# Attention and feed-forward on one core: a shared reciprocal in the prologue, a maximum set free of a remainder, and a copy moved to ScalarE

## The chip, the cores and the metric

The kernel runs on one core of a Trainium2 chip. The metric is the device time of one execution in microseconds (us), taken as the median of several executions. Five engines share the core and run their own instruction streams in order: TensorE (PE, with its weight loads shown apart as PEld), VectorE (DVE), ScalarE (ACT), GpSimd (POOL, hardly used here) and SyncE (SP), whose queue issues most of the DMA transfers. An engine that waits for a semaphore holds everything behind it in its own stream.

## The reference: attention through 32 memory slots, then a gated feed-forward

The inputs have 8 batch elements, 8 heads, 576 positions and head size 64; `phi` has 32 columns for each head and position. Cut to what matters:

```python
a = exp(phi - max(phi, axis=2));  a = a / (sum(a, axis=2) + 1e-9)     # max and sum over the 576 positions
k_m = einsum('bhsm,bhsd->bhmd', a, k);  v_m = einsum('bhsm,bhsd->bhmd', a, v)
scores = scale * (q @ k_m.T)                                          # 576 x 32 for each head
attn = exp(scores - max(scores, axis=-1));  attn = attn / (sum(attn, axis=-1) + 1e-9)
x = (attn @ v_m), heads side by side                                  # 4608 x 512
h = x @ w_in;  out = (h * sigmoid(h)) @ w_out                         # 512 -> 2048 -> 512
```

## The kernel before, in words

The kernel goes through the eight batch elements, numbered 0 to 7. `v_m` and `w_in` are multiplied first (`p_mm`, giving `pm`), so that a batch element's hidden row `h` is attention weights times `pm`. Every float32 operand of a large product is split in a rounded high part and a remainder, both in a 32-bit format that PE takes at full rate, and three products (high x high, high x low, low x high) are summed. In the text "g" is the activated hidden block: `gbuf` holds it as float32, and `gparts` holds its high part (a CAST on DVE in batch elements 0 and 1, line 718) and its remainder (a subtraction on DVE, line 720).

For batch elements 0 and 1 the hidden dimension is done in 16 slots of 128 columns. In a slot PE does `ffn1` (12 products into the PSUM tile `h`, line 701), ACT applies SiLU in two pieces (`gbuf`, line 728; `gleft`, line 730), DVE splits the result, and PE then does the second product of the slot before (`acc`, line 746). `h` has one buffer: `ffn1` of the next slot waits until ACT has read `h` to the end, that is until `gleft`.

Into these slots, as events, is woven the attention of the next batch element. In batch index 1 the next one is element 2, and its events are: the maximum over `phi` (`phi_max`, lines 258 to 261, then `phi_fold`, lines 286 to 304, ending in the tile `am`), its subtraction (`phi_sub`, lines 312 and 315), the exponential on ACT, the products with `k` and `v` (`e_mm`), the turn of their result (`e_tr`, two PE transposes and two copies into `kvT`, lines 368 and 369), and the scores. Batch index 1 also prepares, eight times, sums of weight blocks for a Strassen-like scheme that the later batch elements use (`w_forms`: a sum of 1024 columns on DVE at line 814, four small ones at lines 818 to 821, a rounding on ACT at line 835, a remainder on DVE at line 836).

The order on DVE is found by the tile scheduler, which moves an instruction ahead where it sees it ready. A dependency without a semaphore (`behind`) pins an instruction after another on the same engine. In batch index 1, events whose function stands in the list `late` are pinned behind `last_split[-1]`, the subtraction that makes the remainder of this slot's g. PE's order is the program's throughout, ACT's from batch index 1 on, and in the prologue both DVE and ACT follow the program.

The prologue does the attention of element 0 with nothing to hide behind. Its softmax over 32 slots is done in two parts, u = 0 (512 columns) and u = 1 (640 columns), of one tile `fsc`: maximum, subtraction, exponential on ACT (line 576), sum (line 580), addition of 1e-9 and reciprocal (lines 581 and 582), product (line 586), then PE transposes (`f_back`, tile `firsta`, line 593). Between them stand steps that put the first weights together from 64-bit words (`w_conv`: step "s" is a shift on DVE, line 176, step "a" an addition on DVE, line 178), and groups of spare PE products (`keep_warm`, line 80) that write to a tile nobody reads.

Of the kernel before, what the change touches and what calls it, by code (L numbers as in the profile page):

```python
# [16 lines left out]
ALU = mybir.AluOpType  # L17
AX = mybir.AxisListType

P = 128  # L20
# [28 lines left out]
def attn_ffn_kernel(  # L49
# [313 lines left out]
    def e_tr(b):  # L363
        pt = beside_h(P) if b <= 2 else banks(b)
        t = sb.tile([P, 2, NR, M], F32, tag="kvT", name=f"kvT{b}", bufs=2)
        for kind in range(2):
            nc.tensor.transpose(pt[kind][:, :P], kvn[:, kind].rearrange("p g d -> p (g d)"), ident)
        nc.vector.tensor_copy(t[:, 0].rearrange("p r m -> p (r m)"), pt[0][:, :P])
        nc.scalar.copy(t[:, 1].rearrange("p r m -> p (r m)"), pt[1][:, :P])
        at[b]["kvT"] = t  # L370

# [183 lines left out]
    def f_sc(u):  # L555
        return f_part(u, "sc", 2 * S)

    def f_groups(x):
        return x.rearrange("p (n m) -> p n m", m=M)
# [16 lines left out]
        nc.scalar.activation(f_sc(u), f_sc(u), AF.Exp, scale=SCALE)  # L576

    def f_sum(u):
        sm = f_part(u, "sm", 2 * S // M)
        nc.vector.tensor_reduce(sm, f_groups(f_sc(u)), op=ALU.add, axis=AX.X)  # L580
        nc.vector.tensor_scalar(sm, sm, EPS, None, op0=ALU.add)
        nc.vector.reciprocal(sm, sm)

# [222 lines left out]
    def w_forms(j, step):  # L806


        if step == 0:
            while len(kept) < 3 * j + 3:  # L810
                keep(*homes_left.pop(0))
            f = at[0]["forms", j] = sb.tile([P, 2, DMODEL], F32, tag="cva", name="wf", bufs=1)
            c = slice(2 * j, 2 * j + 2)
            i = nc.vector.tensor_tensor(f, as_f32(wo_hi[:, c]), as_f32(wo_lo[:, c]), op=ALU.add)  # L814
            if j < 3:
                behind(i.ins, last_kvn[0] if j == 2 else last_split[-1])
            b11, b12, b21, b22 = (f[:, k, q * Q : (q + 1) * Q] for k in range(2) for q in range(2))
            nc.vector.tensor_tensor(b11, b12, b11, op=ALU.subtract)
            nc.vector.tensor_tensor(b12, b22, b12, op=ALU.add)
            nc.vector.tensor_tensor(b22, b22, b11, op=ALU.add)  # L820
            nc.vector.tensor_tensor(b21, b22, b21, op=ALU.subtract)
            return
        f = at[0]["forms", j].rearrange("p k (q f) -> p (k q) f", q=2)
        t1 = sb.tile([P, 1, DMODEL], F32R, tag="cva1", name="t1", bufs=1)
        runs = [[t1, 0, 1]]
        for u in range(3 * j, 3 * j + 3):
            t, i = kept_at[u]
            if t is runs[-1][0]:
                runs[-1][2] = i + 1
            else:  # L830
                runs.append([t, i, i + 1])
        n = 0
        for t, i, e in runs:
            src, to = f[:, n : n + e - i], t[:, i:e]
            nc.scalar.activation(to[:, :, :Q], src, AF.Copy)
            nc.vector.tensor_tensor(to[:, :, Q:], src, to[:, :, :Q], op=ALU.subtract)  # L836
            n += e - i
        load(saved[j], as_f32(t1[:, 0]))
# [313 lines left out]
    with in_order(DVE, ACT) as last:  # L1152
        load_phi(0)
        nc.scalar.activation(tiny[:, :1], ident[:, :1], AF.Exp)
        load_kv(0)
        for c in LOADS.split():
            if c[0] == "Q":
                load_q(0, int(c[1]), True)
            elif c[0] == "L":
                load_next(True)  # L1160
            else:
                w_load((c[0], 0), int(c[1]), True)
        keep_warm(idle, 10)
        phi_max(0, (0,))
        phi_allmax(0, (0,))
        phi_max(0, (1,))
        keep_warm(idle, 3)
        phi_sub(0, (0,))
        phi_allmax(0, (1,))
        phi_sub(0, (1,))  # L1170
        for p in range(2):
            phi_exp(0, (p,))
        keep_warm(idle, 2)
        e_mm(0)
        w_conv(I0, 0, "pc")
        keep_warm(idle, 3)
        f_tr()
        f_vt()
        w_conv(I0, 0, "s")
        keep_warm(idle, 2)  # L1180
        f_scores(0)
        f_scores(1)
        f_copy(0)
        w_conv(I0, 0, "a")
        f_turn(0)
        f_copy(1)
        f_max(0)
        f_turn(1)
        f_sub(0)
        spare = ps.tile([P, 512], F32, tag="acc", name="spare", bufs=NI)  # L1190
        keep_warm(spare, 3)
        f_exp(0)
        w_conv(I0, 1, "pc")
        f_max(1)
        f_sub(1)
        f_exp(1)
        nc.scalar.activation(tiny[:, :1], ident[:, :1], AF.Silu)
        keep_warm(spare, 13)
        f_sum(0)
        f_norm(0)  # L1200
        w_conv(I0, 1, "sa")
        f_back(0)
        f_sum(1)
        w_conv(O0, 0, "p")
        f_high(0)
        w_conv(O0, 0, "c")
        keep_warm(spare, 3)
        bg = p_mm(0, 0, CW, False)
        keep_warm(spare, 5)
        p_split(0, 0, CW, bg, (0,))  # L1210
        w_conv(I1, None, "p")
        f_norm(1)
        f_back(1)
        f_low(0)
        w_conv(O0, 0, "s")
        f_high(2)
        p_split(0, 0, CW, bg, (1,))
        f_high(1)
        w_conv(O0, 0, "h")
        f_low(1)  # L1220
        f_low(2)
        w_conv(O0, 0, "a")
        w_conv(I1, None, "c")
        h = ffn1(0, 0, low_last=True)
        g32 = silu(0, 0, h)
        w_conv(I1, None, "s")
        gs = split(g32, steps=(2,))
        w_conv(O0, 0, "l")
        w_conv(I1, None, "a")
        split(g32, steps=(1,), gs=gs)  # L1230
        g32 = silu(0, 1, ffn1(0, 1, bgtile()))
        w_conv(O0, 1, "pc")
        main_step(0, 0, gs, (0, 1), (0, 1))
        g1 = split(g32, steps=(0,))
        w_conv(O0, 1, "s")
        p_mm(0, CW, CW)
        w_conv(O0, 1, "h")
        main_step(0, 0, gs, (0, 1), (2,))
        main_step(0, 0, gs, (2, 3))
        split(g32, steps=(1,), gs=g1)  # L1240
        w_conv(O0, 1, "al")
        prev = ("main", 0, 1, g1)
# [46 lines left out]
    for b in range(B):  # L1289
        if b == 1:  # L1290
            whole.close()
            ctx.enter_context(in_order(ACT))
        for s in range(NFC if b > 1 else 0):
            t, j = divmod(s, NP)
            h = ffn1s(b, t, j)
            part = forms(b, t, j, h)
            run(b, s)
            finish(range(NI))
            prev = ("st", b, t, j, part)
        for fc in range(NFC if b < 2 else 0):  # L1300
            if b == 0 and fc < 2:
                for part in range(2):
                    for fn, a in events.pop((b, fc + part / 2), []):
                        fn(*a)
                continue
            h = ffn1(b, fc, low_last=b == 1 and fc == 0)
            gs = split(silu(b, fc, h), steps=(2, 1) if fc == NFC - 1 else (0, 1))
            for part in range(2):
                if b == 0:
                    finish((2 * part, 2 * part + 1))  # L1310
                traced = nc.cur_bb.bb.instructions
                n = len(traced)
                late = set()
                for fn, a in events.pop((b, fc + part / 2), []):
                    m = len(nc.cur_bb.bb.instructions)
                    fn(*a)
                    if fn is phi_max or b and fn in (s_max, s_sub, s_sum, s_norm, s_back, s_low):
                        late.update(i.name for i in list(nc.cur_bb.bb.instructions)[m:])
                if b == 0:
                    for i in list(nc.cur_bb.bb.instructions)[n:]:  # L1320
                        if i.engine == ACT:
                            behind(i, last_silu[-1])
                        elif i.engine == DVE and (fc > 10 or i.name in late):
                            behind(i, last_split[-1])
                for i in list(nc.cur_bb.bb.instructions)[n:] if b else ():
                    if i.engine == DVE and i.name in late:
                        behind(i, last_split[-1])
            if b:
                finish(range(NI))
            prev = ("main", b, fc, gs)  # L1330
        if b % 2:
            for n in range(NLS):
                gs = left_split(b, n)
                run(b, NFC + n)
                finish((0, 1, 2, 3))
                prev = ("left", b, n, gs)
# [56 lines left out]
```

## Time and profile before

| what | value |
|---|---|
| median of 3 runs | 682.2 us (681.66 to 682.36) |
| the profiled execution | 681.68 us, of which the profile spans 679.9 us |
| PE busy | 666.5 us, 98% of the span |
| DVE, ACT busy | 518.6 us (76%), 370.1 us (54%) |
| granted PE clock over the execution | 0.997 |

PE is busy nearly always, so the row that matters is not a share but the list of the few places where PE stands still. A row of the timeline gives the start, the busy time, the engine, the line, the operation, the tiles, the count, and in brackets the idle time of that engine just before with what ended it. The granted clock is a column of the table by windows: 1.00 is full speed.

### The profile page before, as it was taken

To read this page: it belongs to the slowest core of one execution; us is meant where nothing else is said; L and a number is where in the kernel's file an instruction comes from. 1 tells how busy PE (TensorE), PEld (TensorE's weight loads), DVE (VectorE), ACT (ScalarE), POOL (GpSimd) and SP (SyncE) were. 2 spreads that over 40 slices of the span, in tenths; PEclk is the share of its full clock that TensorE was granted. 3 is DMA by queue.
4 is the path that set the end of the run, shared out by engine and by line. 5 is a ranking of instruction groups with operands and counts; after the bars stand their busy time and mean duration, and the time that the engine had idled before them with its cause. 6 is when DMAs were issued, how large, how long until landed. Compare 5 with 4: busy or idle time off the path is not lost.

```text
span 679.9 us, 14538 instructions
## 1 busy us (share of the span) xinstructions
PE 666.5 (98%) x5792; PEld 589.8 (87%) x5792; DVE 518.6 (76%) x1093; ACT 370.1 (54%) x685; POOL 0.7 (0%) x6
## 2 busy tenths in 40 slices
PE   7999999899999999999999999999999999999997
PEld 3687778687879998999988999899996999889996
DVE  4997897888958688868877678887977668867653
ACT  3878684433535646554654646564654546554541
POOL 0000000000000000000000000000000000000000
PEclk9999999899999999999999999999999999999999
DMA  9998975133271443243430524216431204210001
GB/s 340 368 339 275 322 294 204 50 110 99 89 252 47 183 157 124 79 143 126 173 132 16 184 73 169 101 35 243 156 125 34 86 2 156 95 45 17 32 1 47
DMA packets 37907, 93.92 MB, mean 138 GB/s; under 512 B 4688, under 2 KB 21456, under 8 KB 34256
## 3 DMA queue, kind: packets, MB, share of 16 engines
q1 hardware_dynamic: 36816, 90.22, 38.1%
q10 hardware_dynamic: 1024, 2.77, 1.0%
q8 instruction: 46, 0.75, 0.5%
q14 instruction: 21, 0.17, 0.1%
HBM read 77.22 MB, written 15.73 MB: 137 GB/s over the span
## 4 chain that ended last, share of the span: by engine, by line
PE 85%; DVE 4%; issue 1%; ACT 1%; DMA 0%; ACTq 0%; DVEq 0%
PE sum L893 36%; PE h L854 22%; PE acc L746 7%; PE h L701 5%; PE lsum L977 5%; PE bg L649 3%; PE accleft L746 2%; PE bg L335 1%; PE bg L382 1%; PE h L335 1%; PE pacc L649 1%; DVE wf L814 1%; DVE kept L836 0%; DMA out<-o 0%; DVE gparts L720 0%
## 5 line engine op out<-in xcount | busy, mean ns | idle before, releaser
L854 PE MATMUL h<-aparts,pm 128*128 128x288 f32 x1152 | 168.5, 295 | 0.0
L854 PEld LDWEIGHTS h<-aparts,pm 128*128 128x128 f32 x1152 | 157.4, 188 | 0.5
L868 ACT ACTIVATE gbuf<-h 128x512 f32<-128x512 f32 x96 | 57.3, 597 | 116.8 <-PE h L854 114.2
L893 PE MATMUL sum<-wo_hi,aparts 128*128 128x256 f32 x384 | 102.3, 289 | 0.0
L893 PE MATMUL sum<-kept,aparts 128*128 128x256 f32 x576 | 100.1, 282 | 0.0
L893 PE MATMUL sum<-wo_lo,aparts 128*128 128x256 f32 x384 | 100.0, 282 | 0.0
L873 DVE TENSOR_TENSOR gbuf<-gbuf 128x256 f32<-128x256 f32 x96 | 40.6, 423 | 69.0 <-ACT gbuf L868 68.6
L882 ACT ACTIVATE aparts<-gbuf 128x512 fp32r<-128x512 f32 x86 | 54.4, 633 | 62.1 <-DVE gbuf L877 62.1
L746 PE MATMUL acc<-wo_hi,gparts 128*128 128x512 f32 x256 | 85.1, 397 | 0.0
L893 PEld LDWEIGHTS sum<-kept,aparts 128*128 128x128 f32 x576 | 82.5, 191 | 0.0
L893 PEld LDWEIGHTS sum<-wo_hi,aparts 128*128 128x128 f32 x384 | 72.7, 189 | 9.8 <-ACT gleft L870 7.5
L884 DVE TENSOR_TENSOR gparts<-gbuf,aparts 128x512 fp32r<-128x512 f32 x86 | 59.6, 693 | 19.6 <-ACT aparts L882 19.6
L893 PE MATMUL sum<-wo_hi,gparts 128*128 128x256 f32 x384 | 73.2, 281 | 0.0
L893 PEld LDWEIGHTS sum<-wo_lo,aparts 128*128 128x128 f32 x384 | 73.1, 190 | 0.0
L893 PE MATMUL sum<-kept,gparts 128*128 128x256 f32 x288 | 65.5, 282 | 0.0
L701 PEld LDWEIGHTS h<-aparts,pm 128*128 128x128 f32 x372 | 52.3, 190 | 10.5 <-ACT gleft L730 4.0
L701 PE MATMUL h<-aparts,pm 128*128 128x288 f32 x372 | 56.8, 302 | 4.0 <-ACT gleft L730 2.9
L893 PEld LDWEIGHTS sum<-wo_hi,gparts 128*128 128x128 f32 x384 | 59.4, 190 | 0.0
L746 PEld LDWEIGHTS acc<-wo_hi,gparts 128*128 128x128 f32 x256 | 48.3, 190 | 11.6 <-issue 1.0
L872 ACT ACTIVATE aparts<-gbuf 128x384 fp32r<-128x384 f32 x96 | 50.4, 525 | 0.0
L746 PE MATMUL acc<-wo_lo,gparts 128*128 128x512 f32 x128 | 49.6, 395 | 0.4 <-DVE wo_lo L182 0.4
L893 PEld LDWEIGHTS sum<-kept,gparts 128*128 128x128 f32 x288 | 47.9, 190 | 0.0
(225 smaller groups left out, 956.9 us busy)
## 6 DMA issues: line engine op xcount, KB each, us to landing
win<-win_saved SPq DMA_DIRECT2D x24, 1024.0 KB, 5.0
kv<-in_kv SPq DMA_DIRECT2D x28, 516.0 KB, 5.0
q<-in_q SPq DMA_DIRECT2D x16, 576.0 KB, 6.3
raw<-in_w_in SPq DMA_DIRECT2D x14, 512.0 KB, 7.6
raw<-in_w_out SPq DMA_DIRECT2D x6, 1024.0 KB, 6.5
win_saved<-win SPq DMA_DIRECT2D x4, 1024.0 KB, 8.6
phi<-in_phi SPq DMA_DIRECT2D x7, 576.0 KB, 8.5
out<-oo SPq DMA_DIRECT2D x26, 128.0 KB, 1.9
```

The costliest lines, as they stand in the source:

```text
L335: nc.tensor.matmul(pt[p][M * r : M * (r + 1), :KVW], e[:, p, c, M * r : M * (r + 1)], kvt[c][:, p, r], start=c == 0, stop=False, skip_grou ...
L649: nc.tensor.matmul((bg[p][M * r : M * (r + 1)] if beside else bg[M * r : M * (r + 1), p, :w]).rearrange("p (k f) -> p k f", f=P), kvT[D * ...
L701: nc.tensor.matmul(h[:, hf, :HALF], wt[:, p, fs], a[:, p, hf * HALF : (hf + 1) * HALF], start=n[hf] == 0, stop=n[hf] == 5, skip_group_chec ...
L746: nc.tensor.matmul(acc[key], gt[:, cs], wt[:, fc], start=fc == 0 and n == 0, stop=fc == NFC - 1 and n == 2)
L854: nc.tensor.matmul(h[:, i, :HALF], wt[:, p, f : f + P], a[:, p], start=n == 0, stop=n == 5)
L868: nc.scalar.activation(gbuf[:, :MAIN].rearrange("p (i f) -> p i f", i=2), h[:, :, :w], AF.Silu)
L872: nc.scalar.activation(hi[:, :3], g[:, 1:4], AF.Copy)
L873: nc.vector.tensor_tensor(g[:, 4:6], g[:, :1].broadcast_to([P, 2, P]), g[:, 1:3], op=ALU.subtract)
L882: nc.scalar.activation(hi[:, 3:], g[:, 4:], AF.Copy)
L884: last_split.append(nc.vector.tensor_tensor(lo[:, 3:], g[:, 4:], hi[:, 3:], op=ALU.subtract))
L893: nc.tensor.matmul(sums[bank][:, place * Q : (place + 1) * Q], gt[:, k], wt, start=bank not in begun, stop=True, skip_group_check=True,)
L977: nc.tensor.matmul(sums[k], part[gt][:, 2 * i + k], wt[:, fc], start=n == 0 and i == 0 and m == 0, stop=True, skip_group_check=True,)
```

## The change

Four edits.

1. Prologue: the sums of both parts are taken first, with the shift of the next weights between them; then one addition and one reciprocal serve all 36 columns; then the products of u = 0 and u = 1, with the weights' addition between them.
2. Batch index 1: `phi_max` is no longer in the list `late` there (it still is in batch index 0), so it isn't pinned behind the remainder of g.
3. Batch index 1: the turned keys of element 2 (first copy of `e_tr`) are copied out of PSUM by ACT in place of DVE.
4. Batch index 1: the sixth `w_forms` (j = 5) is pinned behind the remainder of `pm` (`last_p[-1]`, line 679).

```diff
@@ e_tr @@
-        nc.vector.tensor_copy(t[:, 0].rearrange("p r m -> p (r m)"), pt[0][:, :P])
+        (nc.scalar.copy if b == 2 else nc.vector.tensor_copy)(t[:, 0].rearrange("p r m -> p (r m)"), pt[0][:, :P])
@@ f_sum @@
-        sm = f_part(u, "sm", 2 * S // M)
-        nc.vector.tensor_reduce(sm, f_groups(f_sc(u)), op=ALU.add, axis=AX.X)
+        nc.vector.tensor_reduce(f_part(u, "sm", 2 * S // M), f_groups(f_sc(u)), op=ALU.add, axis=AX.X)
+
+    def f_rec():
+        sm = first["sm"]
         nc.vector.tensor_scalar(sm, sm, EPS, None, op0=ALU.add)
         nc.vector.reciprocal(sm, sm)
@@ w_forms @@
-            if j < 3:
-                behind(i.ins, last_kvn[0] if j == 2 else last_split[-1])
+            if j < 3 or j == 5:
+                behind(i.ins, last_kvn[0] if j == 2 else last_p[-1] if j == 5 else last_split[-1])
@@ the prologue @@
         f_sum(0)
+        w_conv(I0, 1, "s")
+        f_sum(1)
+        f_rec()
         f_norm(0)
-        w_conv(I0, 1, "sa")
+        w_conv(I0, 1, "a")
         f_back(0)
-        f_sum(1)
         w_conv(O0, 0, "p")
@@ the loop over batch indices 0 and 1 @@
-                    if fn is phi_max or b and fn in (s_max, s_sub, s_sum, s_norm, s_back, s_low):
+                    if fn is phi_max and not b or b and fn in (s_max, s_sub, s_sum, s_norm, s_back, s_low):
                         late.update(i.name for i in list(nc.cur_bb.bb.instructions)[m:])
```

Only DVE and ACT change their order; PE's and SP's streams are the same instruction for instruction. What follows shows three places.

DVE in the prologue, before (`fsc` is the softmax tile, `fsm` its sums, `win_72` the first weights):

```order
L580 TENSOR_REDUCE fsm<-fsc 128x16
L581 TENSOR_SCALAR fsm<-fsm 128x16
L582 RECIPROCAL fsm<-fsm 128x16
L586 TENSOR_TENSOR fsc<-fsc,fsm 128x512
L176 TENSOR_SCALAR win_72<-win_72 128x512
L178 ISA win_72<-raw,win_72 128x1024
L580 TENSOR_REDUCE fsm<-fsc 128x20
L581 TENSOR_SCALAR fsm<-fsm 128x20
L582 RECIPROCAL fsm<-fsm 128x20
L586 TENSOR_TENSOR fsc<-fsc,fsm 128x640
```

and the same place now (lines are two or so further down):

```order
L579 TENSOR_REDUCE fsm<-fsc 128x16
L176 TENSOR_SCALAR win_72<-win_72 128x512
L579 TENSOR_REDUCE fsm<-fsc 128x20
L583 TENSOR_SCALAR fsm<-fsm 128x36
L584 RECIPROCAL fsm<-fsm 128x36
L588 TENSOR_TENSOR fsc<-fsc,fsm 128x512
L178 ISA win_72<-raw,win_72 128x1024
L588 TENSOR_TENSOR fsc<-fsc,fsm 128x640
```

Two instructions are gone. The product of u = 0 now stands behind the sum of u = 1, and the product of u = 1 has two instructions fewer ahead of it.

DVE at the start of batch index 1, before (`mt`, `mx` belong to `phi_max` of element 2, `pm` is the remainder of a `p_mm`):

```order
L720 TENSOR_TENSOR gparts<-gbuf,gparts 128x512
L718 CAST gparts<-gbuf 128x512
L720 TENSOR_TENSOR gparts<-gbuf,gparts 128x512
L718 CAST gparts<-gbuf 128x512
L720 TENSOR_TENSOR gparts<-gbuf,gparts 128x512
L258 TENSOR_TENSOR mt<-phi_1109 128x512
L259 TENSOR_TENSOR mx<-mt 128x256
L261 TENSOR_TENSOR mx<-mx,phi_1109 64x128
L679 TENSOR_TENSOR pm<-bg,pm 128x1024
L261 TENSOR_TENSOR mx<-mx,phi_1109 64x128
```

and now, up to the same remainder `pm`, from the same first row on (`phi_fold`'s rows between `mxt` and `am`, and `phi_sub`'s, are in the second piece):

```order
L722 TENSOR_TENSOR gparts<-gbuf,gparts 128x512
L258 TENSOR_TENSOR mt<-phi_1107 128x512
L259 TENSOR_TENSOR mx<-mt 128x256
L261 TENSOR_TENSOR mx<-mx,phi_1107 64x128
L720 CAST gparts<-gbuf 128x512
L261 TENSOR_TENSOR mx<-mx,phi_1107 64x128
L722 TENSOR_TENSOR gparts<-gbuf,gparts 128x512
```

and further down the same stream, from the end of `phi_fold` to the first `w_forms`:

```order
L304 STREAM_TRANSPOSE am<-wide 128x256
L312 TENSOR_TENSOR phi_1107<-phi_1107,am 128x512
L315 TENSOR_TENSOR phi_1107<-phi_1107,am 64x128
L720 CAST gparts<-gbuf 128x512
L312 TENSOR_TENSOR phi_1107<-phi_1107,am 128x512
L722 TENSOR_TENSOR gparts<-gbuf,gparts 128x512
L315 TENSOR_TENSOR phi_1107<-phi_1107,am 64x128
L681 TENSOR_TENSOR pm<-bg,pm 128x1024
L720 CAST gparts<-gbuf 128x512
L722 TENSOR_TENSOR gparts<-gbuf,gparts 128x512
L816 TENSOR_TENSOR wf<-wo_hi,wo_lo 128x1024
```

`phi_max` starts two splits of g earlier, `phi_fold` stands whole between the first and the second of these splits, and `phi_sub` ends ahead of the first `w_forms` (`wf`); before, three of its four instructions stood among the rows of that `w_forms`.

DVE in the tenth slot of batch index 1, before (`kvT_1652` are the turned keys of element 2):

```order
L718 CAST gparts<-gbuf 128x512
L814 TENSOR_TENSOR wf<-wo_hi,wo_lo 128x1024
L720 TENSOR_TENSOR gparts<-gbuf,gparts 128x512
L679 TENSOR_TENSOR pm<-bg,pm 128x1024
L368 COPY kvT_1652<-h 128x128
L818 TENSOR_TENSOR wf<-wf 128x256
```

and now, the copy having gone to ACT, where it stands just ahead of the copy of line 369:

```order
L720 CAST gparts<-gbuf 128x512
L722 TENSOR_TENSOR gparts<-gbuf,gparts 128x512
L681 TENSOR_TENSOR pm<-bg,pm 128x1024
L816 TENSOR_TENSOR wf<-wo_hi,wo_lo 128x1024
L820 TENSOR_TENSOR wf<-wf 128x256
```

## The prediction, made before the changed kernel ran

> **What bounds the kernel now.** I read the page first, then PE's own list of waits, then the timeline around each wait that the change touches.
>
> ```profile
> PE 666.5 (98%) x5792; PEld 589.8 (87%) x5792; DVE 518.6 (76%) x1093; ACT 370.1 (54%) x685; POOL 0.7 (0%) x6
> PE h L701 <- ACT gleft L730: 2.9, 1, 2.9
> PE firsta L593 <- DVE fsc L586: 0.7, 2, 0.5
> PE firstm L276 <- DVE cm L271: 1.2, 2, 0.8
> ```
>
> PE bounds it. It stands still only in the prologue and at a handful of places, so a change on DVE or ACT is worth what it does to those waits. The rows (engine, waited for: total, times, longest) name two that the edits touch: 2.9 us at one `ffn1` that waits for `gleft`, and the transposes of the prologue, which wait for the softmax products; a third comes below. The last row is of the prologue too: its longest wait is 0.8 us.
>
> **Edit 2, the maximum set free.** This is where the 2.9 us come from:
>
> ```profile
> 104.55 0.33 SPq L88 DMA_DIRECT2D phi<-in_phi  x1
> phi<-in_phi SPq DMA_DIRECT2D x1, 576.0 KB, 3.8
> 113.00 0.43 DVE L718 CAST gparts<-gbuf 128x512 fp32r<-128x512 f32 x1 [3.13 <-ACT gbuf L728]
> 114.14 0.68 DVE L258 TENSOR_TENSOR mt<-phi 128x512 f32<-128x512 f32 x1
> 121.71 1.22 DVE L814 TENSOR_TENSOR wf<-wo_hi,wo_lo 128x1024 f32<-128x1024 f32 x1
> 123.49 0.42 ACT L835 ACTIVATE t<-wf 128x256 fp32r<-128x256 f32 x1 [5.26 <-DVE wf L818]
> 125.93 0.84 ACT L835 ACTIVATE kept<-wf 128x768 fp32r<-128x768 f32 x1 [2.02 <-DVE wf L821]
> 127.16 0.21 ACT L730 ACTIVATE gleft<-h 128x64 f32<-128x64 f32 x1
> 115.74 1.75 PE L701 MATMUL h<-aparts,pm 128*128 128x288 f32 x12
> 120.07 1.75 PE L701 MATMUL h<-aparts,pm 128*128 128x288 f32 x12
> 127.42 2.60 PE L701 MATMUL h<-aparts,pm 128*128 128x288 f32 x12 [2.86 <-ACT gleft L730]
> 133.40 1.75 PE L701 MATMUL h<-aparts,pm 128*128 128x288 f32 x12
> 128.00:132.00 4.00, 4.00 (x16) 3.56 (x15) 3.63 (x7) 3.72 (x6) 0.00 (x0) 0.57 0.00 0
> ```
>
> Read it backwards. PE's `ffn1` at 127.42 waited 2.86 us for `gleft`. ACT was late with `gleft` because it is in order and stood first at `t`, then at `kept`, for the sums of the first `w_forms` on DVE. DVE was late with those because `mt` started only at 114.14, behind a CAST for which DVE had idled 3.13 us. Yet `phi` was there: issued at 104.55, 3.8 us to landing, at 108.35. The last row (window; busy times of PE, PEld, DVE, ACT, POOL; granted clock, 0.57) shows a second price: after the gap the clock was low.
>
> Now the new time. `mt` can start at about 108.4, when `phi` lands. Between `mt` and `wf` DVE was busy without a gap for 121.71 - 114.14 = 7.57 us. In the new order the same work stands there, and in addition two CASTs, two remainders of g, one large and two small parts of `phi_sub`:
>
> ```profile
> L720 DVE TENSOR_TENSOR gparts<-gbuf,gparts 128x512 fp32r<-128x512 f32 x32 | 22.0, 688 | 1.2 <-PE acc L746 0.5
> L312 DVE TENSOR_TENSOR phi<-phi,am 128x512 f32<-128x512 f32 x12 | 8.2, 681 | 0.0
> L315 DVE TENSOR_TENSOR phi<-phi,am 64x128 f32<-64x128 f32 x12 | 3.4, 284 | 0.2
> ```
>
> With the CAST's 0.43 that is 2 x (0.43 + 0.69) + 0.68 + 2 x 0.28 = 3.48 us, so `wf` starts at 108.4 + 7.57 + 3.48 = 119.45 in place of 121.71. From `wf` to `kept` on ACT it took 125.93 - 121.71 = 4.22 us, with 0.68 + 2 x 0.28 = 1.24 us of `phi_sub` in between that are no longer there: 3.0 us, up to 3.2 as neighbours overlap a little. `kept` starts at 122.4 to 122.6, and `gleft` ends 127.37 - 125.93 = 1.44 us later, at 123.9 to 124.1.
>
> PE, running freely, repeats a slot in 120.07 - 115.74 = 4.33 us and would issue its `ffn1` at 124.40. So `gleft` is 0.4 us early and the whole wait goes: 127.42 - 124.40 = 3.02 us. Without the gap the clock should stay up: 133.40 - 127.42 = 5.98 us for this slot become 4.33, another 1.65 us. Together **-4.67 us**.
>
> Is it given back?
>
> ```profile
> 159.47 1.22 DVE L679 TENSOR_TENSOR pm<-bg,pm 128x1024 fp32r<-128x1024 f32 x1
> 135.88 0.43 DVE L718 CAST gparts<-gbuf 128x512 fp32r<-128x512 f32 x1 [1.46 <-ACT gbuf L728]
> ```
>
> The second CAST and remainder of g now stand behind the maximum and `phi_fold`, and feed PE. Counted back from `wf` at 119.45 over what stands between (a CAST and a remainder 1.1, the remainder of `pm` 1.2, a small `phi_sub` 0.3), that remainder ends at about 116.8. PE takes it up behind the `ffn1` of 115.74, whose row ends at 117.49, so the cover is 0.7 us; beyond it a microsecond on DVE is one on PE. The remainder of `pm` ends near 118.3; its columns are first used by the `ffn1` at 124.4. Behind that slot PE is 4.67 us earlier and DVE only 2.26 + 1.24 = 3.5; the 1.2 us between them fit in DVE's idle time of 1.46 us two slots on.
>
> [...]
>
> **Edits 3 and 4, the tenth slot.**
>
> ```profile
> 157.21 1.03 ACT L677 ACTIVATE pm<-bg 128x1024 fp32r<-128x1024 f32 x1
> 157.73 1.22 DVE L814 TENSOR_TENSOR wf<-wo_hi,wo_lo 128x1024 f32<-128x1024 f32 x1
> 160.17 0.39 PE L746 MATMUL acc<-wo_hi,gparts 128*128 128x512 f32 x1
> 160.92 0.27 ACT L369 COPY kvT<-h 128x128 f32<-128x128 f32 x1 [2.68 <-DVE kvT L368]
> 161.23 1.86 PE L701 MATMUL h<-aparts,pm 128*128 128x288 f32 x12 [0.67 <-ACT kvT L369]
> ```
>
> The transposed keys lie in columns of `h`, so `ffn1` waited for both copies, and DVE reached its copy only behind `wf` and the remainder of `pm` (ended at 160.69); ACT idled 2.68 us for it. ACT is free at 158.24; two copies of 0.27 end by 158.8, long before PE is through with its products of 160.17. The wait of the last row goes: **-0.67 us**. The remainder of `pm`, at 159.47 until now, comes ahead of the 1.22 us of `wf`; and `wf`, later by as much, is next needed by ACT's `t`, which stands behind the next `gleft`, an `ffn1` away (161.23 + 1.86). So edit 4 costs nothing; without that cover it would cost up to 1.2 us.
>
> **Edit 1, the prologue.**
>
> ```profile
> 19.32 0.68 DVE L580 TENSOR_REDUCE fsm<-fsc 128x16 f32<-128x512 f32 x1
> 19.50 0.73 ACT L576 ACTIVATE fsc<-fsc 128x640 f32<-128x640 f32 x1
> 20.53 0.69 DVE L586 TENSOR_TENSOR fsc<-fsc,fsm 128x512 f32<-128x512 f32 x1
> 21.68 0.69 DVE L178 CUSTOM_DVE_ANT_0 win<-raw,win 128x1024 uint16<-128x1024 uint16 x1
> 22.29 0.81 DVE L580 TENSOR_REDUCE fsm<-fsc 128x20 f32<-128x640 f32 x1
> 23.35 0.28 DVE L582 RECIPROCAL fsm<-fsm 128x20 f32<-128x20 f32 x1
> 23.66 0.83 DVE L586 TENSOR_TENSOR fsc<-fsc,fsm 128x640 f32<-128x640 f32 x1
> 100.21 0.38 DVE L440 RECIPROCAL ssm<-ssm 128x36 f32<-128x36 f32 x1
> 17.23 3.62 PE L80 MATMUL spare<-ident 128*128 128x512 bf16 x16
> 21.37 0.63 PE L593 MATMUL firsta<-ident,fsc 128*128 128x128 f32 x4 [0.53 <-DVE fsc L586]
> 23.17 1.25 PE L80 MATMUL spare<-ident 128*128 128x512 bf16 x5
> 24.64 0.63 PE L593 MATMUL firsta<-ident,fsc 128*128 128x128 f32 x4 [0.21 <-DVE fsc L586]
> ```
>
> The second sum can start when its exponential ends (20.23) and the shift is out of the way, at 20.3. From sum to product took 23.66 - 22.29 = 1.37 us; the reciprocal of 36 columns is 0.10 longer: the product of u = 0 starts at 21.77, not 20.53, **1.24 us later**. The product of u = 1, behind it and the addition (22.29 - 21.68 = 0.6 us each), starts at 23.0, 0.6 us earlier. DVE gains, but PE is in order: its first transposes move to 22.6, and behind them stand spare products, a `p_mm` and five more spares before the second transposes. That stretch lasts at least 24.30 - 21.37 = 2.93 us (five spares at 0.226, the mean distance of the sixteen) and at most 24.42 - 21.37 = 3.05. The second transposes come at 25.5 to 25.65 in place of 24.64: **+0.9 to +1.0 us**, and the first `ffn1`, released through them, moves along. PE's list of waits has nothing long behind it until batch index 1, so I find nothing that gives it back. I take +0.9; the bounds are 0 (hidden after all) and the lost clock below.
>
> **The sum.** -4.67 - 0.67 + 0.9 = -4.44 us. The profiled execution took 681.68 us, so it becomes 677.2. It stood 0.5 us under the median of 682.2; the median becomes **677.8 us**.
>
> **Rivals.**
>
> *A wait remains at `gleft`* (13%). The margin is 0.3 to 0.5 us over some 30 DVE instructions. If these take 1.6 us more, PE waits 1.2 us, too short to lose the clock: 679.0. Against it: the sum used unshortened durations.
>
> *The clock falls in the prologue* (11%). PE would stand still from 17.23 + 3.62 = 20.85 to 22.6, 1.75 us. A gap of 2.86 us lost the clock, the 0.8 us of the first fence did not. If this one does, it costs what the other cost, 1.65 us: 679.4. [...]
>
> *`phi` lands late, and the kernel becomes slower* (5%).
>
> ```profile
> phi<-in_phi SPq DMA_DIRECT2D x7, 576.0 KB, 8.5
> ```
>
> Over all seven loads the median is 8.5 us. With it `mt` starts at 113.05 and holds the splits of g behind it: `gleft` at 128.7 in place of 127.37, the clock lost as before, the prologue's 0.9 on top: 681.68 + 1.3 + 0.9 - 0.7 = 683.2, some 683.7 as a median. It decides from a landing of about 7 us on, where the gap is again 2.9 us. Against it: the row for this very load, in a quiet queue, says 3.8.
>
> *The prologue's delay is hidden* (11%), in a later wait of PE that DVE, 0.5 us ahead by the saved pair, answers sooner: 676.9.
>
> *The order does nothing for the time* (2%): 682.2.
>
> **How the numbers follow.** The forecast gets 58%. Range 676.6 to 679.7: from the hidden prologue to the lost clock, which leaves out late `phi`, no effect and accidents. The median can tell about 0.2%, 1.4 us, from no change; below 680.8 lie the forecast and three rivals, 93%, cut to 0.90 for what I don't see; the same 0.05, slower 0.05.
>
> **What would show it.** No PE wait for `gleft` near 124 us and a granted clock of 1.00 in the four microseconds after; `mt` within a microsecond of 109 (all plus the prologue's shift); `ffn1` of the eleventh slot without a wait for `kvT`; the first transposes of the prologue near 22.6 with idle time of about 1.7 us ahead, the second near 25.5 with none. I am wrong if PE waits for `gparts` around 117, if the prologue's clock falls below 1.00, or if the second transposes are no later than 24.64.

## The result and the profile after

The changed kernel takes **677.71 us** (median of 6 executions, 676.74 to 679.49) against 682.12 us of the kernel before (6 executions, 680.09 to 682.72): a ratio of 0.9941, with a 95% interval of 0.9924 to 0.9958. The forecast was 677.8. The profiled execution of the changed kernel spans 675.9 us at a mean granted clock of 1.0, against 679.9 us at 0.997.

PE's line of the page in the changed kernel (in it the lines are two further down: `ffn1` is L703, `gleft` L732):

```profile
PE 664.9 (98%) x5792; PEld 588.8 (87%) x5792; DVE 518.2 (77%) x1090; ACT 370.3 (55%) x686; POOL 0.7 (0%) x6
```

PE is busy 1.6 us less with the same 5792 products: time that the lowered clock, 0.50 over 3.42 us of the trace of before (shown below), had added. Two waits have left the list, the 2.9 us of `ffn1` for `gleft` and its 0.7 us for `kvT`, and one has grown: the transposes of the prologue now wait 1.75 us, once, where they waited 0.7 in two pieces.

**Batch index 1.** The timeline of the changed kernel around the wait that is gone, and one row of its table by windows (window; busy times of PE, PEld, DVE, ACT, POOL; granted clock; DMA):

```profile
105.89 0.33 SPq L88 DMA_DIRECT2D phi<-in_phi  x1
109.74 0.69 DVE L258 TENSOR_TENSOR mt<-phi 128x512 f32<-128x512 f32 x1 [0.83 <-DMA phi<-in_phi]
120.79 1.22 DVE L816 TENSOR_TENSOR wf<-wo_hi,wo_lo 128x1024 f32<-128x1024 f32 x1
124.25 0.85 ACT L837 ACTIVATE kept<-wf 128x768 fp32r<-128x768 f32 x1 [1.34 <-DVE wf L823]
125.48 0.22 ACT L732 ACTIVATE gleft<-h 128x64 f32<-128x64 f32 x1
129.99 0.22 ACT L732 ACTIVATE gleft<-h 128x64 f32<-128x64 f32 x1
117.09 1.75 PE L703 MATMUL h<-aparts,pm 128*128 128x288 f32 x12
121.42 1.75 PE L703 MATMUL h<-aparts,pm 128*128 128x288 f32 x12
125.75 1.86 PE L703 MATMUL h<-aparts,pm 128*128 128x288 f32 x12
130.26 1.86 PE L703 MATMUL h<-aparts,pm 128*128 128x288 f32 x12
128.00:132.00 4.00, 4.00 (x23) 3.24 (x21) 3.86 (x10) 3.31 (x7) 0.00 (x0) 1.00 0.05 20
```

`mt` starts as `phi` lands (its bracket), 3.85 us after its issue, and everything up to `gleft` follows sooner. Seen from the `ffn1` two slots ahead of the one that waited (115.74 before, 117.09 now), `wf` starts at +3.70 in place of +5.97. The `ffn1` at 125.75 comes one free slot of 4.33 us after the one at 121.42, where it came 127.42 - 120.07 = 7.35 us after: -3.02 us. The clock stays at 1.00, where it was 0.57, and the next slot takes 130.26 - 125.75 = 4.51 us in place of 5.98: -1.47. Together -4.49 us.

But `gleft` ends at 125.70 and PE starts at 125.75: there is no margin here, and the 4.51 us of the next slot are 0.18 above a free one. They are ACT's: from one `gleft` to the next it is 129.99 - 125.48 = 4.51 us, since the exponential over `phi` (1.17 us) stands between them, with a table load of 1.28 us on either side of it.

**The tenth slot**: the transposes of the kernel before, and then the timeline of the changed kernel:

```profile
157.37 0.44 PE L367 MATMUL h<-ident,kvn 128*128 128x128 f32 x2 [0.37 <-ACT gleft L730]
```

```profile
154.35 0.44 PE L367 MATMUL h<-ident,kvn 128*128 128x128 f32 x2 [0.38 <-ACT gleft L732]
155.23 0.30 ACT L369 COPY kvT<-h 128x128 f32<-128x128 f32 x1
157.38 1.75 PE L703 MATMUL h<-aparts,pm 128*128 128x288 f32 x12
```

The second copy, on ACT like the first, is through at 155.53, long before PE asks. From the transposes to `ffn1` it is 3.03 us; it was 161.23 - 157.37 = 3.86.

**The prologue**: two rows of `ffn1` in the kernel before (the first and the second slot), then the timeline of the changed kernel, and its clock:

```profile
25.85 2.10 PE L701 MATMUL h<-aparts,pm 128*128 128x288 f32 x12 [0.47 <-DVE aparts L612]
32.98 1.76 PE L701 MATMUL h<-aparts,pm 128*128 128x288 f32 x12
```

```profile
19.91 0.67 DVE L579 TENSOR_REDUCE fsm<-fsc 128x16 f32<-128x512 f32 x1
23.55 0.82 DVE L588 TENSOR_TENSOR fsc<-fsc,fsm 128x640 f32<-128x640 f32 x1
23.18 0.63 PE L595 MATMUL firsta<-ident,fsc 128*128 128x128 f32 x4 [1.75 <-DVE fsc L588]
26.07 0.60 PE L595 MATMUL firsta<-ident,fsc 128*128 128x128 f32 x4
27.25 2.10 PE L703 MATMUL h<-aparts,pm 128*128 128x288 f32 x12 [0.47 <-DVE aparts L614]
34.37 1.76 PE L703 MATMUL h<-aparts,pm 128*128 128x288 f32 x12
19.50:23.50 4.00, 2.25 (x12) 1.04 (x11) 3.90 (x8) 3.36 (x6) 0.00 (x0) 1.00 1.06 380
```

The two executions had not reached the first sum at the same time (19.32 and 19.91), so intervals are compared and not starts. From the first sum to the first transposes it is 3.27 us in place of 21.37 - 19.32 = 2.05, so 1.22 more; to the second transposes 6.16 in place of 5.32, 0.84 more; to the first `ffn1` 27.25 - 19.91 = 7.34 in place of 25.85 - 19.32 = 6.53, so 0.81 more. The `ffn1` of the second slot, at 34.37, keeps it: it stands 14.46 us behind the first sum, where it was 13.66 (it started at 32.98). On DVE the product of u = 1 starts sooner, 23.55 - 19.91 = 3.64 us behind the first sum in place of 23.66 - 19.32 = 4.34; PE makes nothing of it. The clock is 1.00 through the gap.

### The profile page after: what moved, and what is told of

It is laid out like the page before. It is cut to its first block, busy times and chain, and to the rows that moved or that the text cites. A ratio compares the mean times of both kernels' runs of the same rounds, so it can differ in the third digit from the quotient of the medians.

```text
span 675.9 us, 14536 instructions
## 1 busy us (share of the span) xinstructions
PE 664.9 (98%) x5792; PEld 588.8 (87%) x5792; DVE 518.2 (77%) x1090; ACT 370.3 (55%) x686; POOL 0.7 (0%) x6
## 4 chain that ended last, share of the span: by engine, by line
PE 91%; DVE 3%; ACT 2%; DMA 2%; issue 1%; ACTq 0%; DVEq 0%; SPq 0%
PE sum L895 36%; PE h L856 23%; PE acc L748 10%; PE h L703 6%; PE lsum L979 5%; PE bg L651 4%; PE accleft L748 2%; PE bg L335 1%; DMA kv<-in_kv 1%; DMA q<-in_q 1%; PE bg L382 1%; PE h L335 1%; PE pacc L651 1%; ACT cva L172 0%; ACT raw L174 0%
## 5 line engine op out<-in xcount | busy, mean ns | idle before, releaser
L703 PEld LDWEIGHTS h<-aparts,pm 128*128 128x128 f32 x372 | 51.7, 188 | 6.7 <-issue 2.7
L703 PE MATMUL h<-aparts,pm 128*128 128x288 f32 x372 | 56.1, 299 | 0.5 <-DVE aparts L614 0.5
```

Of the source, the lines that this page charges most:

```text
L703: nc.tensor.matmul(h[:, hf, :HALF], wt[:, p, fs], a[:, p, hf * HALF : (hf + 1) * HALF], start=n[hf] == 0, stop=n[hf] == 5, skip_group_chec ...
```

## The experiments

The theory was that of the forecast: edit 2 takes away a wait and a loss of clock at one place, edits 3 and 4 take away one short wait, and edit 1 costs what it delays on PE. The rivals: edit 1 is hidden later; the clock is lost in the prologue's longer gap; the gain at `gleft` comes from the wait alone, and the clock falls for another reason.

### Edit 1 alone

The kernel before, with the new prologue (the split of `f_sum`, as in the diff of the change, is left out here):

```diff
         f_sum(0)
+        w_conv(I0, 1, "s")
+        f_sum(1)
+        f_rec()
         f_norm(0)
-        w_conv(I0, 1, "sa")
+        w_conv(I0, 1, "a")
         f_back(0)
-        f_sum(1)
```

> The kernel before with edit 1 alone. My theory (PE's stream is in order, so what stands behind the first transposes moves with them): the prologue is longer. From the start of the first sum on DVE to the start of the first ffn1 it was 6.53 us before and is 7.34 us in the changed kernel; it should be 7.3 to 7.4 here, nothing should give it back, and the time should be 0.8 to 0.9 us above the kernel before. The rival (hidden): the interval is longer, yet the waits of PE behind it shrink and the time is the same within 0.2 us. A second rival (the saved pair on DVE helps): the time falls by up to 0.5 us.

Measured: 682.48 us (12 executions) against 681.73 (23 of the kernel before), a ratio of 1.0008 (0.9998 to 1.0019). Timeline of this kernel, and one row of its windows:

```profile
21.03 0.68 DVE L579 TENSOR_REDUCE fsm<-fsc 128x16 f32<-128x512 f32 x1
28.36 1.83 PE L703 MATMUL h<-aparts,pm 128*128 128x288 f32 x10 [0.47 <-DVE aparts L614]
129.96 1.85 PE L703 MATMUL h<-aparts,pm 128*128 128x288 f32 x12 [2.82 <-ACT gleft L732]
134.47 1.86 PE L703 MATMUL h<-aparts,pm 128*128 128x288 f32 x12
11.00:12.00 1.00, 1.00 (x21) 0.86 (x24) 0.30 (x2) 0.94 (x2) 0.00 (x0) 0.50 1.07 380
```

28.36 - 21.03 = 7.33 us, the same as in the changed kernel: +0.80 on the trace. The interval of the ratio holds zero, since the executions of both kernels fall in groups by their mean granted clock. Within a group they can be compared: at 1.000, 681.27 to 681.93 (4 executions) against 679.97 to 681.0 (4); at 0.997 (or 0.996) a median of 682.7 (8) against 681.7 (16). That is +0.9 to +1.0 in both.

The clock here was not lost in the prologue's new gap (1.00 from 22 to 26 us). Two things surprise: it was at 0.50 at 11 us (last row), before anything that edit 1 touches, and it was *not* lost at the gap of 2.82 us, whose next slot took 134.47 - 129.96 = 4.51 us. The fourth experiment takes that up.

### The change without edit 1

The changed kernel, with the prologue of before: the diff above, reversed.

> The changed kernel with edit 1 undone, edits 2 to 4 kept. My theory: 0.8 to 0.9 us faster than the changed kernel, that is 5.2 us faster than the kernel before (some 677.0 where that takes 682.2), with the interval from the first sum to the first ffn1 back at 6.5 us. The rival (hidden): the same time as the changed kernel. Also a test of whether the gain of edits 2 to 4 depends on edit 1, which I don't expect.

Measured: 676.78 us (676.39 to 677.38, 6 executions), a ratio of 0.993 (0.9914 to 0.9946); measured again later, on another chip (the expectation stands with the last experiment), 676.76 (4 executions). On its timeline:

```profile
19.25 0.67 DVE L580 TENSOR_REDUCE fsm<-fsc 128x16 f32<-128x512 f32 x1
25.77 2.09 PE L701 MATMUL h<-aparts,pm 128*128 128x288 f32 x12 [0.47 <-DVE aparts L612]
```

6.52 us, as before the change, and 677.71 - 676.78 = 0.93 us less than the whole change. From both sides edit 1 costs 0.9 us. Nothing later gives it back.

### Edit 2 alone

```diff
-                    if fn is phi_max or b and fn in (s_max, ...):
+                    if fn is phi_max and not b or b and fn in (s_max, ...):
```

> The kernel before with edit 2 alone (the maximum over phi free in batch index 1). My theory: this edit carries the gain. The wait of 2.86 us for gleft goes, the granted clock stays at 1.00 behind it, and the ffn1 one slot later starts 4.5 us earlier against the slots before; the time falls by 4.4 to 4.7 us. The wait for kvT of 0.67 us stays. Rival: edits 2 and 4 need each other, since both reorder the same block preparations, and the gain alone is under 3 us.

Measured: 677.41 us (677.3 to 678.31, 4 executions), a ratio of 0.9941 (0.9922 to 0.9959): 4.3 us of the gain against 681.73 of the kernel before, measured beside it. On its timeline:

```profile
119.88 1.75 PE L701 MATMUL h<-aparts,pm 128*128 128x288 f32 x12
124.56 1.85 PE L701 MATMUL h<-aparts,pm 128*128 128x288 f32 x12 [0.18 <-ACT gleft L730]
157.00 1.87 PE L701 MATMUL h<-aparts,pm 128*128 128x288 f32 x12 [0.66 <-ACT kvT L369]
```

The wait for `kvT` is still there, as it should be. A rest of the wait for `gleft` is also there, 0.18 us, and the slot is 4.68 us long. The step from here to the change without edit 1 is what edits 3 and 4 give: 677.41 - 676.78 = 0.63 us, from 4 and 6 executions whose ranges touch.

### The clock's part, taken apart from the wait's

The kernel before, with twelve spare products, written to a tile that nobody reads, between the second products and the `ffn1` that waits. The wait for `gleft` stays, but PE has something to do in it:

```diff
+            if b == 1 and fc == 4:
+                keep_warm(bgtile()[:, 0], 12)
             h = ffn1(b, fc, low_last=b == 1 and fc == 0)
```

> The kernel before with 12 spare products on PE (results unread) put into the gap of 2.86 us that it has ahead of the fifth ffn1 of batch index 1, so that the wait for gleft stays and only PE's idleness goes. This parts the two prices of the gap. My theory: the ffn1 still starts near 127.4 us but the granted clock stays at 1.00, the slot behind takes 4.3 to 4.5 us in place of 5.98, and the time falls by about 1.6 us. Rival (the slow products came from something else than idleness, such as a wait or a port): the slot still takes 6 us and the time does not change.

Measured: 680.2 us (680.04 to 680.94, 10 executions), a ratio of 0.9979 (0.9969 to 0.9989). On its timeline and in its windows:

```profile
124.87 2.76 PE L80 MATMUL bg<-ident 128*128 128x512 bf16 x12
128.04 1.85 PE L701 MATMUL h<-aparts,pm 128*128 128x288 f32 x12 [0.41 <-ACT gleft L730]
132.55 1.86 PE L701 MATMUL h<-aparts,pm 128*128 128x288 f32 x12
128.00:132.00 4.00, 3.96 (x22) 3.57 (x23) 3.79 (x7) 3.95 (x4) 0.00 (x0) 1.00 0.01 4
```

`ffn1` comes as late as ever, 7.53 us after the one before it (7.35 before), but the clock is 1.00 and the next slot is 132.55 - 128.04 = 4.51 us long in place of 5.98, which is 1.47 less. The median falls by 681.73 - 680.2 = 1.5 us; by the two intervals it would be 1.47 - 0.18 = 1.3. So here PE's idle time is what cost the clock (behind 2.86 us of it the clock fell to 0.50, behind 0.41 us it stayed at 1.00, and all 10 executions ran at 0.999 or 1.000), and of the gain of edit 2 about 3.0 us are the wait and 1.5 the clock.

That price is not paid in every execution. The kernel before ran 40 times beside these experiments, in three series: 28 times at a mean granted clock of 0.996 or 0.997 (681.12 to 682.6 us), 8 times at 1.000 (679.97 to 681.0) and 4 times at 0.994 (682.83 to 684.1). The medians of the three groups are 1.6 and 1.7 us apart, about one slowed stretch (1.47 us on the trace) each. In the kernels without the long gap (the whole change, this one, and all others here with edit 2) 44 of 45 executions ran at 0.999 or 1.000. So it is that gap which usually, but not always, costs the clock, and a stretch can also be lost elsewhere, as the profile of edit 1 alone shows (0.50 at 11 us).

The lowered stretch in the trace of before, cut to fit it:

```profile
128.22:131.64 3.42, 3.42 (x13) 3.03 (x13) 3.28 (x6) 3.14 (x4) 0.00 (x0) 0.50 0.00 0
```

Half the clock over 3.42 us. Three other traces here have a lowered stretch, and by the clocks of their windows each lasts about 3.4 us: edit 3 alone and edit 4 alone (below), both behind the same gap, and edit 1 alone, from about 9.5 to 12.9 us.

In the three traces that lost the clock behind the gap (2.86 us long before, 2.72 in edit 3 alone and in edit 4 alone), it falls 0.5 to 0.8 us after the gap's end. In the trace of edit 1 alone the gap is as long, 2.82 us, and the clock stays at 1.00 behind it. What decides between the two no run shows, and how much idle time is enough was not tested.

### The spare products in front of the transposes

The forecast gave the reason of edit 1's cost as PE's order: three and five spare products and a `p_mm` stand behind the first transposes, so a delay of these delays the second. The test moves the spares, all eight, ahead of the first transposes, where PE now idles for 1.75 us:

```diff
         w_conv(I0, 1, "a")
+        keep_warm(spare, 8)
         f_back(0)
         w_conv(O0, 0, "p")
         f_high(0)
         w_conv(O0, 0, "c")
-        keep_warm(spare, 3)
         bg = p_mm(0, 0, CW, False)
-        keep_warm(spare, 5)
```

> The changed kernel with the 3 and the 5 spare products that stand between the first and the second transposes of the prologue moved ahead of the first ones, where PE idles 1.75 us. My theory (the order costs time only because PE has spares queued between): the second transposes start as soon as the product of u = 1 is there, about 1.5 us earlier, but ACT's preparation of weights stands ahead of the rounding of that half, so ffn1 gains about 0.7 us; the time falls 0.7 us below the changed kernel. Rival (the prologue's length is set by DVE or ACT alone): no change within 0.2 us.

Measured: 676.86 us (676.33 to 678.5, 6 executions), a ratio of 0.9932 (0.9917 to 0.9947) to 682.0 us of the kernel before, measured beside it. On its timeline:

```profile
22.74 0.63 PE L595 MATMUL firsta<-ident,fsc 128*128 128x128 f32 x4
24.08 0.63 PE L595 MATMUL firsta<-ident,fsc 128*128 128x128 f32 x4
26.61 1.72 PE L703 MATMUL h<-aparts,pm 128*128 128x288 f32 x10 [0.70 <-ACT aparts L616]
```

The gap in front of the first transposes is filled and the second follow them by 1.34 us, where it was 26.07 - 23.18 = 2.89. By the medians, which are of different series, 677.71 - 676.86 = 0.85 us are back. On the trace it is less: the `ffn1` of the second slot stands 13.88 us behind the first sum, where it was 14.46 in the changed kernel and 13.66 before, so 0.58 of 0.80 are back. The rest is ACT's: `ffn1`, started early, is stopped by it with ten of its products left (last row). So edit 1 did shorten DVE's chain (the products of the softmax end sooner), and PE's order wasted it.

A second version also moves ACT's first step on the next weights behind `f_high(1)`, which is what stopped `ffn1`:

```diff
-        w_conv(I1, None, "p")
         f_norm(1)
         f_back(1)
...
         w_conv(O0, 0, "h")
+        w_conv(I1, None, "p")
```

> As the run with the spares ahead, and in addition ACT's first step on the next weights (1.13 us) moved behind the rounding of the second half and of the first output weights. My theory: ffn1 of the first slot starts 1.5 us earlier than in the changed kernel; the SiLU behind it gains about 1.0 us because ACT still has the moved step to do; the time is about 1.0 us under the changed kernel, some 676.7 where that takes 677.7. Rival: the moved step is late for the second weights and PE waits at the p_mm behind the first ffn1s, so that the gain is under 0.5 us.

Measured: 676.78 us (676.35 to 677.13, 5 executions), a ratio of 0.9928 (0.9916 to 0.9941). On its timeline:

```profile
25.36 2.10 PE L703 MATMUL h<-aparts,pm 128*128 128x288 f32 x12 [0.59 <-DVE aparts L614]
32.99 1.75 PE L703 MATMUL h<-aparts,pm 128*128 128x288 f32 x12
```

`ffn1` now runs through, 5.93 us after the first sum at 19.43, which is 0.6 us sooner than in the kernel before; but the second product then waits 0.27 us for ACT. Of the 0.6 us only 0.1 is left at the `ffn1` of the second slot (last row): 13.56 us after the first sum, where it is 13.66 in the kernel before. So with both moves the loss is gone on the trace too, but the new prologue gains nothing that can be told: the change without edit 1 also takes 676.78.

### Edit 3 alone, and edit 4 alone

One execution of each: the kernel before with only the copy on ACT, and with only the pin.

```diff
-        nc.vector.tensor_copy(t[:, 0]..., pt[0][:, :P])
+        (nc.scalar.copy if b == 2 else nc.vector.tensor_copy)(t[:, 0]..., pt[0][:, :P])
```

> The kernel before with edit 3 alone (the copy on ACT, the sixth block preparation where it was). My theory: this edit alone takes the wait for kvT away; the interval from the first products of that slot (the two transposes) to the next ffn1 falls from 3.86 to about 3.0 us. Rival: without edit 4 the remainder of pm, which stays behind the block sums on DVE until 160.7 us, becomes the new wait at the products of the scores, and PE loses part of it there.

```diff
-            if j < 3:
-                behind(i.ins, last_kvn[0] if j == 2 else last_split[-1])
+            if j < 3 or j == 5:
+                behind(i.ins, last_kvn[0] if j == 2 else last_p[-1] if j == 5 else last_split[-1])
```

> The kernel before with edit 4 alone (the sixth block preparation pinned behind the remainder of pm, the copy still on DVE). In DVE's order the copy then stands ahead of the remainder of pm. My theory: the copy comes about 2 us earlier, so this edit alone takes the wait for kvT away too, and edits 3 and 4 are two ways to the same 0.67 us, not two gains: the interval from the two transposes to the next ffn1 is about 3.0 us here as well. Rival: only the move to ACT helps and the interval stays at 3.86 us.

Measured: 681.04 and 681.15 us, one execution each, too few to tell 0.6 us. The timelines tell it; first of edit 3 alone, then of edit 4 alone:

```profile
157.64 0.44 PE L367 MATMUL h<-ident,kvn 128*128 128x128 f32 x2 [0.37 <-ACT gleft L730]
160.67 1.75 PE L701 MATMUL h<-aparts,pm 128*128 128x288 f32 x12
```

```profile
158.96 0.28 DVE L368 COPY kvT<-h 128x128 f32<-128x128 f32 x1
160.84 1.75 PE L701 MATMUL h<-aparts,pm 128*128 128x288 f32 x12
```

In both `ffn1` follows the transposes by 3.03 us (the transposes of the second start at 157.81) and waits for nothing. With `wf` pinned back (it starts at 160.29), DVE reaches its copy at 158.96, early enough without ACT. The late remainder of `pm`, the rival for edit 3, holds nothing: the slot from this `ffn1` to the next takes 5.74 us there, as in the changed kernel. The two edits are two ways to the same 0.6 to 0.8 us; together they give it once.

### Where the 0.18 us at `gleft` come from

The forecast left 0.3 to 0.5 us of margin; the runs show none. Between the first `wf` and `kept` a remainder (`t`, line 836) stands on DVE between the second and the third of the small sums, and `kept` waits for the fourth. The change without edit 1, with that remainder pinned behind the fourth sum:

```diff
-            nc.vector.tensor_tensor(b21, b22, b21, op=ALU.subtract)
+            at[0]["sum", j] = nc.vector.tensor_tensor(b21, b22, b21, op=ALU.subtract)
...
-            nc.vector.tensor_tensor(to[:, :, Q:], src, to[:, :, :Q], op=ALU.subtract)
+            r = nc.vector.tensor_tensor(to[:, :, Q:], src, to[:, :, :Q], op=ALU.subtract)
+            if j == 0 and n == 0:
+                behind(r.ins, at[0]["sum", j])
```

> The kernel with edits 2, 3 and 4 and the old prologue, and in the first `w_forms` of batch index 1 the remainder of `t` moved behind the fourth small sum on DVE (before: between the second and the third). Theory A (the margin at `gleft` is what was mis-sized: the chain from the first sum of 1024 columns through the small sums and `kept` to `gleft` is the last to arrive): `kept` starts one remainder, 0.34 us, sooner, 3.1 us after `wf` instead of 3.46; the slot of the `ffn1` that waited 0.18 us for `gleft` falls from 4.52 to 4.33 us, the next from 4.51 to 4.33, and the time falls by 0.2 to 0.4 us, to about 676.4. Theory B (the 0.18 us is something else, such as ACT's fixed interval from one `gleft` to the next or PE's own pace): `kept` is earlier and both slots stay at 4.5 us; the time stays at 676.8.

and beside it, unchanged:

> The same kernel without that move, on the same chip in the same call, so that a few tenths of a microsecond can be compared: both theories expect 676.8 with slots of 4.52 and 4.51 us; a difference of more than 0.3 us from 676.78 would be the scatter from call to call.

Measured: 676.29 us (676.12 to 676.75, 4 executions) against 676.76 (676.36 to 677.34, 4). On the timeline with the move, and then without it:

```profile
119.47 1.22 DVE L814 TENSOR_TENSOR wf<-wo_hi,wo_lo 128x1024 f32<-128x1024 f32 x1
122.62 0.85 ACT L835 ACTIVATE kept<-wf 128x768 fp32r<-128x768 f32 x1 [1.01 <-DVE wf L821]
120.09 1.75 PE L701 MATMUL h<-aparts,pm 128*128 128x288 f32 x12
124.42 1.75 PE L701 MATMUL h<-aparts,pm 128*128 128x288 f32 x12
128.76 1.75 PE L701 MATMUL h<-aparts,pm 128*128 128x288 f32 x12
```

```profile
119.68 1.22 DVE L814 TENSOR_TENSOR wf<-wo_hi,wo_lo 128x1024 f32<-128x1024 f32 x1
123.15 0.85 ACT L835 ACTIVATE kept<-wf 128x768 fp32r<-128x768 f32 x1 [1.33 <-DVE wf L821]
120.36 1.75 PE L701 MATMUL h<-aparts,pm 128*128 128x288 f32 x12
129.16 1.86 PE L701 MATMUL h<-aparts,pm 128*128 128x288 f32 x12
```

From `wf` to `kept` it is 3.15 us with the move and 3.47 without. The two slots from the `ffn1` near 120 take 8.67 us (two free ones of 4.33) against 8.80. Theory A holds: the sums on DVE arrived last. But what theory B names is there too. From one `gleft` to the next ACT takes 4.5 us in both (123.85 to 128.35 with the move, 124.38 to 128.88 without), more than PE's 4.33; with the move `gleft` is through 0.35 us before PE asks, which covers the difference once, and without it 0.09, which doesn't. On the trace that is 0.13 us here (0.36 against the first run of the same kernel, whose slots were 4.52 and 4.51); the medians differ by 0.47, and with 4 executions each, whose spreads overlap, at most its sign is worth something. This version, with the old prologue, is the fastest of the study: a ratio of 0.992 (0.9892 to 0.9949) to before.

## Why the prediction was right, point by point

- **Edit 2, the wait (-3.02).** Right to the hundredth: -3.02 on the trace. `mt` started as `phi` landed, and `wf` came 2.27 us earlier against PE's slots, where 121.71 - 119.45 = 2.26 was forecast.
- **Edit 2, the margin.** The step that failed is "from `wf` to `kept` 3.0 us, up to 3.2": it measured 3.46. Three `phi_sub` instructions of together 1.24 us were taken away, and the stretch fell by only 4.22 - 3.46 = 0.76. The timeline of before, and then that of the changed kernel, has the instruction behind `wf`:

```profile
122.85 0.28 DVE L315 TENSOR_TENSOR phi<-phi,am 64x128 f32<-64x128 f32 x1
```

```profile
122.04 0.42 DVE L820 TENSOR_TENSOR wf<-wf 128x256 f32<-128x256 f32 x1
```

  Before, a piece of `phi_sub`, which needs nothing of `wf`, started at 122.85, before `wf` ended (121.71 + 1.22 = 122.93). Now a sum stands there that reads `wf`, and starts at 122.04, after it ended (120.79 + 1.22 = 122.01). Two of the three removed instructions had started 0.08 us before the row ahead of them ended, and the row behind each started 0.07 to 0.08 us before its end; the rows' busy times, 1.24 us added up, were more than the 0.76 us that they took. So the margin at `gleft` was about 0 and not 0.3 to 0.5, and slots here are up to 0.35 us longer than free ones (4.68 in edit 2 alone). Moving one remainder out of that stretch removed this. That the whole wait went even so is in part luck: `gleft` came 0.05 us ahead of the `ffn1` in the changed kernel, and 0.35 us too late in edit 2 alone.
- **Edit 2, the clock (-1.65).** That the gap costs the clock is right, shown by filling it (1.00 in place of 0.57 from 128 to 132 us); the size is 1.47, since the slot behind fell to 4.51 and not to 4.33. That is ACT's interval from `gleft` to `gleft`, which the forecast left out: it shows as soon as the margin is under 0.18 us. And the price is one of most executions, not of all: 32 of 40 of the kernel before lost at least one stretch. The median lies in the group that lost one, so the whole price counts in it; the one profile before the change could not show that.
- **Edits 3 and 4 (-0.67, and nothing).** -0.83 by the starts, -0.63 by the times of two kernels. That edit 4 costs nothing is right, but it was read only as a cost: alone it removes the same wait.
- **Edit 1 (+0.9).** +0.81 on the trace, 0.93 by the kernel without it, with the reason that was given, PE's order: with the spares ahead of the transposes most of the loss is gone, and with ACT's step moved too all of it. DVE did get through the softmax 0.7 us sooner (0.6 was forecast); in that order nobody could use it.
- **The sum.** On the trace -4.49 - 0.83 + 0.81 = -4.5 us, forecast -4.44. By the medians of the experiments, -4.32 for edit 2, -0.63 for edits 3 and 4, +0.93 for edit 1: -4.02; compared directly, 677.71 - 682.12 = -4.41. That the median came out within 0.1 us of the forecast is in part luck: the errors of the three terms on the trace (+0.18, -0.16, -0.09) nearly cancel, and the median of the kernel before moved between 681.73 and 682.12 from series to series.

The rivals. *A wait remains at `gleft`* is true in small, 0.2 us (in edit 2 alone) where the rival had 1.2. It took these 1.2 us as too short to lose the clock, an estimate between the 0.8 us that kept it and the 2.86 that lost it; no run had such a wait there, and 1.75 us in the changed kernel's prologue left the clock at 1.00. *The clock falls in the prologue* did not happen: the gap came, at 1.75 us, and the clock stayed at 1.00 in the profile, with 0.999 or more in all 6 executions. *The prologue's delay is hidden* is refuted by both experiments on edit 1. *`phi` lands late* did not happen in this profile, where it took 3.85 us from its issue; how late it could land at other times was not tried. What the forecast named as its refutation, a wait for `gparts` around 117 us, did not come.

## What to carry to other kernels

When an instruction is taken out of a stretch, the stretch need not fall by its duration where its neighbours depend on one another (here by 0.76 us for rows of 1.24): measure such a stretch from start to start, and give a margin that hangs on it that much less. A saving on one engine reaches the end only through the order of the next: whatever stands on PE between two of its results (spare products above all) turns an earlier second result into nothing and a later first one into a loss (here 0.7 us sooner on DVE, 0.9 us lost in time). And a wait of PE should be priced with the clock behind it (here about 3.0 and 1.5 us): fill it with spare products once, and the two prices come apart.

## What the runs showed of the hardware that was not expected

- A gap of 2.7 to 2.9 us on PE lost the clock in most executions of one and the same program, not in all: by their mean granted clock the 40 executions of before fall in steps of 1.6 us (8 at 1.000, with none lost; 28 at 0.996 or 0.997, with one; 4 at 0.994, with two), and one profile, that of edit 1 alone, has the gap of 2.82 us with the clock at 1.00 behind it. The stretch at half clock lasts about 3.4 us in all four traces that have one (3.42 in that of before).
- The clock was lost around smaller gaps too: in the profile of edit 1 alone it was at 0.50 from about 9.5 to 12.9 us, behind waits of PE of 0.88, 0.38 and 0.78 us within 3.7 us. The last two are in the profiles of the kernel before and of the changed kernel as well, the first, for a tile of the maximum (`mx`), is not. Together these waits are 2.04 us, less than the gap of 2.82 us behind which the same profile keeps 1.00, and the single gap of 1.75 us in the changed kernel's prologue lost nothing; so why the clock fell there stays open.
